# Five feed-forward slices ahead instead of three in the first block, and no attention loads in the first step of a burst

## The chip, the cores and the metric

The kernel runs as one program on one core of a Trainium2 chip. The metric is the device time of one execution in microseconds (us). The core's engines are TensorE (PE in the profile; PEld is its weight load), VectorE (DVE), ScalarE (ACT), GpSimd (POOL) and SyncE (SP, which here only issues DMAs). Each engine runs its own instructions in program order and waits on semaphores for the others.

## The reference

Chunked attention without a mask, followed by two gated feed-forward blocks. Batch, heads, sequence and head size are 8, 8, 576 and 64; the chunk is 64; there are 4608 tokens of width 512.

```python
attn = softmax(scale * q_c @ k_c^T)      # per chunk of 64 tokens and head
x = (attn @ v_c) as tokens x 512
x = ((x @ w_a) * (x @ w_b)) @ w_out      # 512 -> 1536 -> 512
x = (((x @ w1) * (x @ w2)) @ w3) @ w_o2  # 512 -> 1024 -> 1024 -> 512
```

## The kernel before, in words

The 4608 tokens are nine blocks of 512. float32 products are made of three fp32r products of parts: a weight or an activation is split into a high part (an ACT copy, line 253) and a low part (a subtraction on DVE or POOL, line 254).

The first feed-forward layer is phase 0. Its width of 1536 is cut into 12 slices `f` (`NF[0]` = 12). Slice `f` needs the pair of weights `w_a`, `w_b` and the output weights `wo`. A weight is loaded as raw doubles (`Conv.load`, line 170), turned into float32 by four operations on DVE and ACT (lines 176, 179, 182, 187: `s1` and `s2`) and split (lines 669, 673; 695, 698 for `wo`). `Pump` keeps these jobs in order, three for a slice: `w_a`, `w_b`, `wo`. The converted weights are stored to DRAM by POOL's queue (line 157): the split pair as `dw` (512 KB each), the unsplit pair as `d32` (256 KB each), `wo` as `dwo`; later blocks load them from there.

The first two blocks, T = 0 and T = 1, are done plainly, slice by slice. Before the first slice the attention of block T = 0 runs for four head pairs (`U[0]` to `U[3]`) in a software pipeline: a step `t` holds `turn` (transposes of q and k on PE, copied out by ACT), `scores`, `soft1` and `soft2` (DVE, with the exponent on ACT), `flip`, `apply` and `put`; five conversion jobs run between them. Then `plain_step` runs the slices in the order of `plain_order`: `AHEAD` slices of T = 0 alone, then T = 1's slice `f - AHEAD` before T = 0's slice `f`, then the rest of T = 1. A step of T = 0 is 24 products of 128x512 (`pa` and `pb`, line 843) and 12 of the layer's second product for the slice before (`acc`, line 886, from `wo`); a step of T = 1 has the 24 only, and its gated result waits in SBUF (`G0p`). At the points within a step a `Track` hands out pieces: the conversions (`conv`) and the attention of T = 1 (`late`) and then of the next two blocks (`at`).

After the two blocks comes a burst: the second products of T = 1, 12 steps of 12 products, each with its `wo` loaded from DRAM by `Outs.ahead`, which has four homes for them. In the burst the operands of the next pair of blocks are formed on DVE and ACT (pieces of `strassen_pieces`). Four more pairs or single blocks of phase 0 and then phase 1 follow, each with a burst.

q, k and v are not loaded where they are asked for: `ask` puts a load in a list, and `tick(loads=n)` hands the next n to SP's queue, one for each quarter of a burst step; a piece that needs its data calls `settle`, which hands out all that stand before them. SP issues in order, so a load that waits for its buffer holds up all that stand behind it.

## Time and profile before

| what | value |
|---|---|
| median of 3 runs | 1638.82 us (1638.47 to 1640.89) |
| profiled execution, its own time | 1642.08 us |
| span of the profiled execution | 1640.3 us |
| granted TensorE clock, mean over the span | 0.986 of full speed |
| HBM traffic | 268.70 MB read, 85.98 MB written |

The span runs from the first to the last instruction; its execution took 1.8 us longer than it, and lies 3.3 us above the median. In the profile's page PE is busy for 1559.8 us of the span; the part that is not is spread unevenly, so the stretches are read one by one. A timeline row gives the start, the length, the line and the operation, and in brackets the idle time ahead of it with what ended it.

### The profile page before, as it was taken

What the parts mean: (1) busy time and instruction counts of PE and PEld (TensorE: products, weight loads), DVE (VectorE), ACT (ScalarE), POOL (GpSimd) and SP (SyncE); (2) the same over time, 40 slices, a digit from 0 to 9 for tenths busy, and PEclk for the clock granted to TensorE, in tenths of its full rate; (3) what the DMA queues carried; (4) which work ended last, traced back from release to release, by engine and by line L of the source; (5) the groups of instructions that cost most, each with busy time, mean ns of one, the idle gap of its engine ahead of it and who ended that gap; (6) DMA issues with size and microseconds to landing.
All of it is one profiled execution on the core that took longest, in us unless ns stands there. A gap on an engine that the chain in (4) does not pass through costs nothing.

```text
span 1640.3 us, 24184 instructions
## 1 busy us (share of the span) xinstructions
PE 1559.8 (95%) x8968; PEld 1254.6 (76%) x8968; DVE 858.3 (52%) x1384; ACT 551.4 (34%) x989; POOL 490.5 (30%) x502
## 2 busy tenths in 40 slices
PE   4889997899998999999999899999999999999998
PEld 3668776677777777787777677888878878878887
DVE  5667756486756555476775235545542442442331
ACT  5545444222343222433234223333421321321322
POOL 1223333222243211442225112223521421421422
PEclk8899998999999999999999999999999999999999
DMA  9977844787726787379984799776366266266184
GB/s 223 291 224 248 273 154 129 227 249 229 251 85 188 202 225 228 106 223 335 343 281 164 270 313 322 307 268 247 118 223 217 75 221 221 71 216 205 67 292 155
DMA packets 277013, 356.31 MB, mean 217 GB/s; under 512 B 174240, under 2 KB 194720, under 8 KB 276896
## 3 DMA queue, kind: packets, MB, share of 16 engines
q1 hardware_dynamic: 249728, 265.63, 52.9%
q0 software_dynamic: 23616, 81.80, 13.0%
q10 hardware_dynamic: 3552, 7.34, 1.3%
q8 instruction: 71, 1.16, 0.3%
q14 instruction: 46, 0.38, 0.1%
HBM read 268.70 MB, written 85.98 MB: 216 GB/s over the span
## 4 chain that ended last, share of the span: by engine, by line
PE 78%; DVE 6%; DMA 5%; issue 3%; ACT 3%; SPq 3%; POOL 1%; DVEq 0%; POOLq 0%; ACTq 0%
PE P L857 40%; PE acc L886 21%; PE pa L843 4%; PE pb L843 4%; PE wf L1115 3%; DMA wo<-dwo 3%; SPq L148 2%; PE pb0L L843 2%; PE pa0L L843 2%; PE x L407 1%; PE s L356 1%; DVE c L945 1%; DMA qk<-in_q_dram 1%; ACT xP L253 1%; PE t L478 1%
## 5 line engine op out<-in xcount | busy, mean ns | idle before, releaser
L857 PE MATMUL P<-xP,w 128*128 128x512 f32 (+1 forms) x3066 | 704.5, 382 | 11.6 <-DVE c L945 8.6
L857 PEld LDWEIGHTS P<-xP,w 128*128 128x128 f32 x3066 | 550.4, 188 | 135.2 <-DVE c L945 13.4
L945 DVE TENSOR_TENSOR c<-P,c 128x512 f32<-128x512 f32 (+1 forms) x228 | 150.4, 662 | 332.6 <-PE P L857 331.9
L942 ACT COPY c<-P 128x512 f32<-128x512 f32 (+1 forms) x228 | 128.4, 564 | 227.4 <-PE P L857 227.1
L973 POOL TENSOR_TENSOR G<-c,c 128x512 f32<-128x512 f32 x68 | 89.7, 1319 | 332.5 <-DVE c L945 332.4
L253 ACT CAST gh<-c 128x512 fp32r<-128x512 f32 x68 | 42.2, 621 | 329.6 <-DVE c L972 329.6
L254 POOL TENSOR_TENSOR gl<-c,gh 128x512 fp32r<-128x512 f32 x68 | 90.7, 1334 | 171.7 <-ACT gh L253 171.7
L886 PE MATMUL acc<-gh,wo 128*128 128x512 f32 x384 | 138.0, 397 | 0.0
L972 DVE TENSOR_TENSOR c<-P,c 128x512 f32<-128x512 f32 x68 | 47.0, 692 | 135.1 <-PE P L857 135.0
L886 PE MATMUL acc<-wo,gh 128*128 128x512 f32 x320 | 111.1, 390 | 0.5 <-ACT gh L253 0.5
L157 POOL DMA_DIRECT2D dw<-w x58 | 32.3, 558 | 176.5 <-DVE w L254 80.2
L886 PEld LDWEIGHTS acc<-gh,wo 128*128 128x128 f32 x384 | 72.5, 189 | 15.8
L254 DVE TENSOR_TENSOR xP<-xP,xP 128x512 fp32r<-128x512 f32 (+1 forms) x56 | 65.1, 1203 | 28.1 <-ACT xP L253 28.1
L843 PE MATMUL pa<-xq,w 128*128 128x512 f32 x288 | 76.0, 416 | 0.0
L886 PE MATMUL acc<-gl,wo 128*128 128x512 f32 x192 | 75.3, 392 | 0.0
L843 PE MATMUL pb<-xq,w 128*128 128x512 f32 x288 | 71.1, 396 | 0.0
L886 PEld LDWEIGHTS acc<-wo,gh 128*128 128x128 f32 x320 | 60.1, 188 | 13.4 <-ACT gh L253 1.0
L895 ACT COPY ev<-acc 128x512 f32<-128x512 f32 x72 | 42.4, 588 | 80.0 <-PE acc L886 75.1
L843 PEld LDWEIGHTS pa<-xq,w 128*128 128x128 f32 x288 | 57.0, 201 | 13.2 <-ACT xq L253 0.3
L886 PE MATMUL acc<-wo,gl 128*128 128x512 f32 x160 | 62.7, 392 | 0.8 <-POOL gl L254 0.8
L843 PEld LDWEIGHTS pb<-xq,w 128*128 128x128 f32 x288 | 52.9, 188 | 10.8
L373 ACT ACTIVATE e<-e 128x512 f32<-128x512 f32 x36 | 22.8, 632 | 90.5 <-DVE e L367 90.5
(158 smaller groups left out, 2369.8 us busy)
## 6 DMA issues: line engine op xcount, KB each, us to landing
w<-dw SPq DMA_DIRECT2D x175, 512.0 KB, 4.6
wo<-dwo SPq DMA_DIRECT2D x128, 512.0 KB, 4.5
dw<-w POOLq DMA_DIRECT2D x58, 512.0 KB, 4.2
w<-dw SPq DMA_DIRECT2D x75, 256.0 KB, 3.8
su<-d SPq DMA_DIRECT2D x20, 512.0 KB, 5.1
x2d<-ev POOLq DMA_DIRECT2D x36, 256.0 KB, 3.7
x<-x2d SPq DMA_DIRECT2D x36, 256.0 KB, 4.7
out_dram<-ev POOLq DMA_DIRECT2D x36, 256.0 KB, 3.0
```

The source lines that it names most:

```text
L148: nc.sync.dma_start(*asks["left"].popleft())
L253: nc.scalar.copy(dst_h, src)
L254: eng_l.tensor_tensor(dst_l, src, dst_h, op=ALU.subtract)
L843: nc.tensor.matmul(ps, w[m][:, kk // 2, wp, kk % 2], xq[kk // 2][:, kk % 2, xp], start=(n == 0), stop=(n == 3 * KM - 1),)
L857: nc.tensor.matmul(ps, w[:, wp, kt], x[:, kt, xp], start=(begins and n == 0), stop=(n == 5), skip_group_check=True,)
L886: nc.tensor.matmul(acc[m], a, b, start=(f == 0 and (wp, gp) == SEQ[0]), stop=(f == NF[ph] - 1 and (wp, gp) == SEQ[-1]),)
L895: nc.scalar.copy(t, acc[m])
L942: nc.scalar.copy(t, src)
L945: add = lambda o, a, b: nc.vector.tensor_tensor(o, a, b, op=ALU.add)
L972: nc.vector.tensor_tensor(g, last, c11, op=ALU.mult)
L973: nc.gpsimd.tensor_tensor(g_place(ph, nm.split("_")[0], f, gplaces), c22, c12, op=ALU.mult)
L1115: nc.tensor.matmul(ps, t[:, gp, jj], wo2[jj // 2][:, jj % 2, wp], start=(jj == 0 and (wp, gp) == SEQ[0]), stop=(jj == NF[1] - 1 and (wp, g ...
```

## The change

Four things change. First, the start: q, k and v of `U[0]` and `U[1]` are loaded on three queues (SP, ACT, POOL), the first three weights are loaded on SP behind them and not ahead of them on ACT, and of the conversion jobs two and not five run ahead of the first slice. Second, the order of the slices: five slices of T = 0 come first, the pair weights of slices 4 and 5 stand in the homes `G1` and `G2`, and the `dw` stores of slice `f + 1` are put out in T = 1's step `f` (those of 0 and 1 in step 0). Third, PE writes the transposes of q and k in token order, every fourth column, so that ACT's copy is contiguous. Fourth, the bursts: no asked load is handed out in step 0 (`hold`), four `wo` are looked at after it, and the loads for the next pair of blocks stand among the burst's pieces and not ahead of the burst.

```diff
     def tick(every=False, loads=0):
-        settle(asks["done"] + loads)
+        settle(asks["done"] + (0 if state.get("hold") else loads))
...
                 for t in range(4):
-                    c = slice(t * P, (t + 1) * P)
-                    nc.tensor.transpose(ps[:, c], src[:, c], ident)
-                nc.scalar.copy(
-                    self.t[i].rearrange("p (i t) -> p t i", t=4),
-                    ps.rearrange("p (t i) -> p t i", t=4),
-                )
+                    nc.tensor.transpose(to[:, t], src[:, t * P : (t + 1) * P], ident)
+                nc.scalar.copy(self.t[i], ps)
...
+        def queues(self):
+            early = self.T == 0 and self.hp < 2
+            return nc.sync, nc.scalar if early else nc.sync, nc.gpsimd if early else nc.sync
...
-            t = w_tile(2 * (f % 4) + m, f"w0_{f}_{m}")
-            pairs.setdefault((0, f), {})[m] = t
+            if f in (4, 5):
+                if m == 0:
+                    tiles = pool.tile([P, 2, 2, 2, 2, P], F32R, tag=f"G{f - 3}", name=f"w0_{f}")
+                    pairs[0, f] = {i: tiles[:, i] for i in range(2)}
+                t = pairs[0, f][m]
+            else:
+                t = w_tile(2 * ((f if f < 4 else f - 6) % 4) + m, f"w0_{f}_{m}")
+                pairs.setdefault((0, f), {})[m] = t
...
-                store(dw[0][f][m], whole(t).bitcast(F32), 2, nc.gpsimd)
...
+        state["hold"] = True
         parts = [ready(ph, j, order[0], gplaces) if first is None else first]
...
                 parts.append(ready(ph, j, order[2], gplaces))
-            state["outs"].ahead(3)
+                state["hold"] = False
+            state["outs"].ahead(3 if f else 4)
...
-        for i in range(3):
-            pump.load(nc.scalar)
-        for u in U[:NHP]:
+        for n, u in enumerate(U[:NHP]):
             u.load1()
             u.load2()
-        settle(asks["all"])
+            settle(asks["all"])
+            if n:
+                pump.load()
...
-                seq += [(1, f - ahead), (0, f)]
-            return seq + [(1, f) for f in range(n - ahead, n)]
-
-        AHEAD = 3
+                upto = f - ahead + 1 if f < 9 else f - 2
+                seq += [(1, i) for i in range(done, upto)] + [(0, f)]
+                done = upto
+            return seq + [(1, f) for f in range(done, n)]
+
+        AHEAD = 5
...
-            if t in (1, 2, 4, 5, 6):
+            if t == 2:
+                pump.ahead = 0
+                pump.begin(2)
+            if t == 3:
                 pump.run()
+                pump.run()
+            if t == 4:
+                pump.flush()
+            if t == NHP + 2:
+                pump.ahead = 2
+                pump.begin(4)
...
-                conv = Track([conv_piece()] * (1 if f == 0 else 3), 5 if f + 1 < AHEAD else 8)
+                conv = Track([conv_piece()] * (4 if f == 0 else 3), 5 if f + 1 < AHEAD else 8)
...
+            if T == 1:
+                for i in [f + 1] if f else [0, 1]:
+                    for m in range(2 if i < NF[0] else 0):
+                        store(dw[0][i][m], whole(pairs[0, i][m]).bitcast(F32), 2, nc.gpsimd)
...
-                    first_sums[n_].load()
-                for n_, i in ((0, 0), (0, 3), (1, 0)):
-                    load_part(ph, orders[ph, sb][n_], i)
+                    begins_with.append((0.1, False, first_sums[n_].load))
+                for n_, i in ((0, 0), (0, 3), (1, 0), (1, 3)):
+                    begins_with.append(
+                        (0.1, False, lambda f=orders[ph, sb][n_], i=i: load_part(ph, f, i))
+                    )
+                for n_, p in enumerate(begins_with):
+                    pieces.insert(4 + 3 * n_, p)
...
-                if sb == 1:
-                    settle(units[0].qk_end)
-                    load_part(ph, orders[ph, sb][1], 3)
```

The first place is the start of SP's queue, where a name as `qk_0_256` is the q and k buffer of head pair 0 with a running number, and `cv` is a raw weight. Before:

```order
L148 DMA qk_0_256<-in_q_dram 128x4x64 x2
L148 DMA qk_0_256<-in_k_dram 128x4x64 x2
L148 DMA v_0_257<-in_v_dram 128x4x64 x2
L148 DMA qk_1_258<-in_q_dram 128x4x64 x2
L148 DMA qk_1_258<-in_k_dram 128x4x64 x2
L148 DMA v_1_259<-in_v_dram 128x4x64 x2
L148 DMA qk_2_260<-in_q_dram 128x4x64 x2
```

On the same queue now, at its start:

```order
L149 DMA qk_0_250<-in_q_dram 128x4x64 x2
L149 DMA qk_1_258<-in_q_dram 128x4x64 x2
L171 DMA cv_Y_266<-in_moe_w_a_dram 128x4x256
L149 DMA qk_2_269<-in_q_dram 128x4x64 x2
L149 DMA qk_2_269<-in_k_dram 128x4x64 x2
L149 DMA v_2_270<-in_v_dram 128x4x64 x2
L171 DMA cv_Y_266<-in_moe_w_b_dram 128x4x256
```

The k and v loads of the first two head pairs have left for ACT's and POOL's queues, and the weights that ACT issued at its start stand here between the head pairs.

The second place is POOL in the first slices; `dw` and `d` are the DRAM homes of the split and the unsplit pair, `gl` the low part that the second product waits for. Before, from the first store:

```order
L157 DMA dw_0_0_64<-w_0_0_350 128x1024
L157 DMA d_0_0_144<-cv_Y_251 128x512
L157 DMA dw_0_1_65<-w_0_1_420 128x1024
L157 DMA d_0_0_144<-cv_Y_251 128x512
L695 TENSOR_TENSOR wo_579<-cv_Y_251,wo_579 128x512
L157 DMA dwo_0_164<-wo_579 128x1024
L157 DMA dw_1_0_68<-w_1_0_629 128x1024
L157 DMA d_0_1_145<-cv_Y_251 128x512
L254 TENSOR_TENSOR gl_0_0_719<-sa_0_0_675,gh_0_0_718 128x512
```

POOL now, from its first store:

```order
L158 DMA d_0_0_144<-cv_Y_267 128x512 x2
L255 TENSOR_TENSOR gl_0_0_693<-sa_0_0_654,gh_0_0_692 128x512
L707 TENSOR_TENSOR wo_657<-cv_Y_267,wo_657 128x512
L158 DMA dwo_0_164<-wo_657 128x1024
L158 DMA d_0_1_145<-cv_Y_267 128x512
L158 DMA d_0_1_145<-cv_xo_344 128x512
L707 TENSOR_TENSOR wo_759<-cv_xo_344,wo_759 128x512
L158 DMA dwo_1_165<-wo_759 128x1024
L255 TENSOR_TENSOR gl_0_1_817<-sa_0_1_784,gh_0_1_816 128x512
```

The `dw` stores are gone from here; the first four of them stand behind the fifth slice's `gl`.

The third place is SP's queue at the end of the first burst, where `wo_0` is the last `wo` of the burst. Before:

```order
L726 DMA wo_2_3190<-dwo_2_166 128x1024
L148 DMA v_1_2900<-in_v_dram 64x2x64 x4
L726 DMA wo_1_3220<-dwo_1_165 128x1024
L148 DMA qk_2_3125<-in_q_dram 32x8x32 x4
L726 DMA wo_0_3246<-dwo_0_164 128x1024
L148 DMA qk_2_3125<-in_q_dram 32x8x32 x4
```

The same stretch now:

```order
L738 DMA wo_2_3166<-dwo_2_166 128x1024
L149 DMA qk_1_2887<-in_q_dram 32x8x32 x4
L738 DMA wo_1_3196<-dwo_1_165 128x1024
L149 DMA qk_1_2887<-in_q_dram 32x8x32 x4
L149 DMA qk_1_2887<-in_k_dram 32x8x32 x8
L149 DMA v_1_2888<-in_v_dram 64x2x64 x2
L738 DMA wo_0_3232<-dwo_0_164 128x1024
```

The attention loads run one head pair later than before, and 14 of them now stand between the last two `wo`, where there were 4.

## Rows read from the trace of the kernel before

**Rows 1.** Stretches, us: busy by PE, PEld, DVE, ACT, POOL; clock, DMA share, GB/s.

```profile
0.00:39.20 39.20, 18.38 (x304) 14.43 (x304) 23.07 (x54) 20.08 (x31) 3.48 (x11) 0.91 0.92 229
39.20:93.10 53.90, 42.43 (x412) 32.24 (x408) 35.64 (x69) 28.16 (x47) 15.22 (x19) 0.88 0.88 269
93.10:261.60 168.50, 165.12 (x1220) 132.89 (x1213) 107.00 (x180) 73.64 (x128) 51.24 (x62) 0.99 0.66 210
261.60:312.80 51.20, 41.15 (x191) 32.52 (x190) 32.49 (x45) 19.86 (x37) 19.77 (x19) 0.87 0.71 195
480.90:521.30 40.40, 37.03 (x191) 29.70 (x190) 32.31 (x38) 18.79 (x34) 20.74 (x18) 1.00 0.58 159
684.40:720.50 36.10, 36.02 (x158) 29.15 (x157) 28.75 (x27) 18.41 (x33) 21.75 (x18) 1.00 0.63 181
```

**Rows 2.** Timeline of PE, from the start to T = 1's first slice.

```profile
8.72 1.08 PE L478 MATMUL t<-ident,qk 128*128 128x128 f32 x4 [8.72 <-DMA qk<-in_q_dram]
...
39.23 4.49 PE L843 MATMUL pa<-xq,w 128*128 128x512 f32 x12
...
77.72 1.04 PE L478 MATMUL t<-ident,qk 128*128 128x128 f32 x8
...
93.11 4.61 PE L843 MATMUL pa<-xq,w 128*128 128x512 f32 x12
```

**Rows 3.** Waits of PE from 0 to 94 us: total, times, longest.

```profile
PE f L491 <- DVE e L381: 10.7, 5, 3.9
```

**Rows 4.** Timeline of DVE: its first instruction.

```profile
13.38 0.76 DVE L365 TENSOR_REDUCE mx<-s 128x4 f32<-128x256 f32 x2 [13.38 <-PE s L356]
```

**Rows 5.** Groups on DVE, 0 to 262 us: count, busy us, mean ns, idle before.

```profile
L187 DVE SCALAR_TENSOR_TENSOR cv_xo<-cv_xo,cv_xo 128x512 int32<-128x512 int32 x16 | 17.6, 1098 | 2.1 <-ACT cv_xo L182 2.1
L179 DVE SCALAR_TENSOR_TENSOR cv_xo<-cv_xo 128x512 int32<-128x512 int32 x16 | 12.0, 753 | 0.8
L381 DVE TENSOR_TENSOR e<-e,sm 128x512 f32<-128x512 f32 x16 | 12.7, 793 | 0.6
L365 DVE TENSOR_REDUCE mx<-s 128x4 f32<-128x256 f32 x32 | 12.0, 417 | 19.6 <-PE s L356 19.6
L378 DVE TENSOR_REDUCE sm<-e 128x8 f32<-128x512 f32 x16 | 10.8, 678 | 2.3 <-ACT e L373 2.3
L669 DVE TENSOR_TENSOR w<-cv_Y,w 128x512 fp32r<-128x512 f32 x13 | 8.9, 685 | 8.1 <-ACT w L673 8.1
L176 DVE TENSOR_SCALAR cv_xo<-cv_xo 128x512 int32<-128x512 uint32 x16 | 8.1, 504 | 0.0
```

**Rows 6.** Groups on ACT, 0 to 262 us, same columns.

```profile
L479 ACT COPY kT<-t 128x512 f32<-128x512 f32 x16 | 17.8, 1114 | 0.7 <-PE t L478 0.6
L494 ACT COPY pT<-f 128x512 f32<-128x512 f32 x16 | 9.5, 591 | 11.8 <-PE f L491 11.8
```

**Rows 7.** The chain that ended last: start, us, what.

```profile
133.36 2.72 PE pa L843 x12
...
289.87 2.72 PE acc L886 x12
```

**Rows 8.** Timeline of PE, the waits of the first two bursts.

```profile
283.18 0.76 PE L886 MATMUL acc<-gh_1b,wo 128*128 128x512 f32 x1 [7.40 <-DMA wo<-dwo]
...
308.35 0.51 PE L886 MATMUL acc<-gh_1b,wo 128*128 128x512 f32 x1 [2.65 <-DMA wo<-dwo]
...
518.42 0.47 PE L886 MATMUL acc<-gh_3b,wo 128*128 128x512 f32 x1 [1.55 <-DMA wo<-dwo]
```

**Rows 9.** Timeline of SP's queue, first burst.

```profile
265.03 5.61 SPq L148 DMA_DIRECT2D qk<-in_k_dram  x8
...
278.92 0.34 SPq L726 DMA_DIRECT2D wo<-dwo  x1
```

**Rows 10.** The chain again: the last `wo` of the first and second burst.

```profile
301.32 6.89 DMA wo<-dwo
...
514.23 4.06 DMA wo<-dwo
```

More of the change, by code (lines that the diff above doesn't have):

```diff
@@ L139, in chunk_attention_two_gated_products, with ask @@
     asks = {"left": deque(), "all": 0, "done": 0}
-    def ask(to, src):
-        asks["left"].append((to, src))
+    def ask(to, src, queue=None):
+        asks["left"].append((queue or nc.sync, to, src))
         asks["all"] += 1
@@ L147, in settle @@
         while asks["done"] < n and asks["left"]:
-            nc.sync.dma_start(*asks["left"].popleft())
+            queue, to, src = asks["left"].popleft()
+            queue.dma_start(to, src)
             asks["done"] += 1
     def tick(every=False, loads=0):
-        settle(asks["done"] + loads)
+        settle(asks["done"] + (0 if state.get("hold") else loads))
         for s in stores:
@@ L436, in chunk_attention_two_gated_products @@
     class TurnedOnPE(Unit):
+        def queues(self):
+            return nc.sync, nc.sync, nc.sync
         def load_qk(self):
@@ L451, in load_qk @@
                             ),
+                            self.queues()[0 if src is q else 1],
                         )
@@ L462, in load_v @@
                             hs[s : s + n, :].rearrange("(c p) d -> p c d", p=P),
+                            self.queues()[2],
                         )
@@ L475, in turn @@
             for i, (ps, src) in enumerate(zip(self.banks("t"), (self.qb, self.kb))):
+                to = ps.rearrange("p (i t) -> p t i", t=4)
                 for t in range(4):
-                    c = slice(t * P, (t + 1) * P)
-                    nc.tensor.transpose(ps[:, c], src[:, c], ident)
-                nc.scalar.copy(
-                    self.t[i].rearrange("p (i t) -> p t i", t=4),
-                    ps.rearrange("p (t i) -> p t i", t=4),
-                )
+                    nc.tensor.transpose(to[:, t], src[:, t * P : (t + 1) * P], ident)
+                nc.scalar.copy(self.t[i], ps)
         def flip_bank(self):
@@ L506, in chunk_attention_two_gated_products, with queues @@
     class First(TurnedOnPE):
+        def queues(self):
+            early = self.T == 0 and self.hp < 2
+            return nc.sync, nc.scalar if early else nc.sync, nc.gpsimd if early else nc.sync
         def slots(self):
@@ L1191, in plain_order @@
         def plain_order(ph, ahead):
-            n = NF[ph]
+            n, done = NF[ph], 0
             seq = [(0, f) for f in range(ahead)]
             for f in range(ahead, n):
-                seq += [(1, f - ahead), (0, f)]
-            return seq + [(1, f) for f in range(n - ahead, n)]
-        AHEAD = 3
+                upto = f - ahead + 1 if f < 9 else f - 2
[3 more added lines that the diff above has]
+        AHEAD = 5
         order = plain_order(0, AHEAD)
@@ L1217, in chunk_attention_two_gated_products @@
                 U[t + 1].load2()
-            if t in (1, 2, 4, 5, 6):
+            if t == 2:
+                pump.ahead = 0
+                pump.begin(2)
+            if t == 3:
                 pump.run()
+                pump.run()
[4 more added lines that the diff above has]
+                pump.begin(4)
             if t < 3:
-                pump.load(nc.scalar)
+                pump.load()
             tick(loads=8)
@@ L1234, in chunk_attention_two_gated_products @@
                 late.finish()
-                at = Track(both[cut:], 4 * (len(order) - n) - 2)
+                at = Track(both[cut:], sum(3 if T_ else 5 for T_, _ in order[n:]) - 3)
             def point(pe=True):
@@ L1386, in chunk_attention_two_gated_products @@
             if ph == 0 and sb == 1:
+                begins_with = []
                 for n_ in range(2):
                     first_sums[n_] = summed(ph, orders[ph, sb][n_], n_)
-                    first_sums[n_].load()
-                for n_, i in ((0, 0), (0, 3), (1, 0)):
-                    load_part(ph, orders[ph, sb][n_], i)
+                    begins_with.append((0.1, False, first_sums[n_].load))
[5 more added lines that the diff above has]
+                    pieces.insert(4 + 3 * n_, p)
                 pieces = pieces + first_sums[0].pieces()
```

## The prediction

> **What bounds the kernel now.** PE is busy for 1559.8 us of the span, so the question is where the other 80 us are. I read the stretches first [rows 1]: from slice to slice of the two plain blocks, between 93.1 and 261.6 us, PE is busy for 165.1 of 168.5 us at a clock of 0.99, and nothing is to be had there. Three stretches are different. Ahead of the first slice it is busy for 18.4 of 39.2 us; in the three slices that T = 0 runs alone for 42.4 of 53.9 us, and then at a clock of 0.88; in the first burst for 41.2 of 51.2 us. The third burst has the same second products and no wait: 36.1 us.
>
> The timeline of PE says what begins and ends them [rows 2]: the first transpose waits for q until 8.72 us, the first slice starts at 39.23, T = 1's first slice at 93.11. The list of waits names the softmax on DVE as the longest of PE's releasers besides that first q, 10.7 us in 5 waits [rows 3]. DVE itself starts at 13.38 us [rows 4] and is busy for 23.07 of the 25.8 us until 39.2. So the start is a load and then a DVE chain; the lone slices are a chain of PE, ACT and DVE that neither engine fills (DVE is busy for 35.6 of 53.9 us, 66%). In the bursts PE waits for `wo`, 7.40 and 2.65 us in the first and 1.55 in the second [rows 8]; SP's queue shows why the first is late: it issues 8 loads of k in 5.61 us, more of v behind them, and the `wo` only at 278.92 [rows 9].
>
> **The change, part by part.** *Start.* Before, 1.5 MB of weights and 0.5 MB of q and k had to land for the first transpose: 2.0 MB at the 229 GB/s of the stretch is 8.7 us, as seen. Now q and k of the first head pair share the DMA only with v and the next q and k, some 1.25 MB: 5.5 us, a gain of 3.2. Two ACT copies of a turn lie on the chain; contiguous they should take what the flip's copy takes, 0.59 for 1.11 us [rows 6]: 1.0. Of the conversions ahead of the last softmax three `s1` (lines 176 and 179, 0.50 + 0.75) and two `s2` (line 187, 1.10) go, 6 us of DVE by the means [rows 5]; I take 4, because these means hold the long cases of later slices. The first slice then starts at 39.2 - 3.2 - 1.0 - 4 = 31 us (28 if all 6 count and the pipeline tightens, 36 if `w_b`, which now lands behind 3.25 MB, about 14 us, holds DVE up).
>
> *Five lone slices.* Demands until T = 1's first slice. DVE: a set of three conversions is 3 x (0.50 + 0.75 + 1.10) + 2 x 0.69 = 8.4 us; five sets are 42 (two jobs are done by the start, 17 are needed by the time T = 1 begins). Four head pairs of attention at 0.68 + 0.79 + three times two half-size instructions of 0.375 + 0.4 for two small ones = 4.1 each are 16.5. Five gated products are 3.4. That is 62 us, and 56 if back-to-back starts save what the 23.07 busy us of the first stretch suggest; I take 58. PE: five slices at 2 x 2.72 and four second products at 2.72 [rows 7] are 38.1; attention is 3.3 per head pair (165.1 busy us less 12 x 5.44 and 9 x 8.16, over eight), so 13.2: 51 us. DMA: until 93.1 us 9.0 + 14.5 = 23.5 MB moved; seven `dw` stores of 0.5 MB leave, two slices with 2.5 MB each of loads, `d32` and `dwo` come: 25 MB, which at 229 and then 269 GB/s end at 98.7 us. DVE at the 0.9 that it reached between 13.4 and 39.2 us gives 31 + 58 / 0.9 = 95 us. All three are near full; I take 95, between 87 (56 us without idle time) and 99. Attention has 25 points now for what had 15, which is why I expect 0.9 and not the 0.66 of before. By 95 us two slices more are done, each 5.44 + 2.72 = 8.16: the gain is 93.1 + 16.3 - 95 = 14.4 us.
>
> *Rest of the two blocks.* The `dw` stores come here: 12 MB in all. T = 1's first step and the slice behind it (16.3 us with attention) meet four of them, 2 MB, with 1.5 MB of weights, 1 MB of other stores and 0.5 MB of attention: 307 GB/s, above the 269 seen. The buffers of slice 0's weights are written again only for slice 6, so most of this is hidden: 1 us (0 to 4).
>
> *Transposes in every fourth column.* 128 of them in the span, eight in 1.04 us, 0.13 each [rows 2]. No row shows PE writing with a stride. Nearest is ACT, whose strided copy takes 1.11 for 0.59 us, 1.9 times [rows 6]; that much on 0.13 is 0.12 x 128 = 15 us, the upper bound; the lower is 0. A transpose of 128 columns takes more than twice what a product takes for as many (2.72 / 12 / 4 = 0.057 us), so its output is slow enough to hide a halved rate: 2 us. The Trainium skill (SBUF — State Buffer, Door 1: The DMA port swizzle) says that PSUM has lines of 8 bytes and that a non-contiguous PSUM access pattern significantly slows matmuls. By that rule the term would lie near the upper bound; no row of this trace shows it.
>
> *First burst.* SP is free when it starts, and `wo_7` goes out as its home comes free, about 2.9 us in. But the asked loads now start one step late and were not handed out ahead, and those of the second head pair are forced by its `turn`: 14 stand before `wo_0`. Ahead of `wo_0` stand 44 asked loads, 8 `wo` and 6 others. At 0.65 us (0.70 in rows 9, where the queue was fuller), 0.4 and 0.37 that is 34 us; with 2.9 to start and 1 for a home it goes out at 37.8 us and lands after 4.1 [rows 10] at 41.9. The last step (2.72) ends at 44.6, and with half the clock behind a wait of 6 us, as behind the 7.40, at 46.6: 4.6 us less than 51.2. Bounds: 13.7 less if no `wo` is late (36.1 and 1.4 for scores), 1.8 less if the landing takes 6.89.
>
> *Second burst.* The same forcing adds 8 asked loads before the last `wo`: 8 x 0.55 = 4.4 us, of which 1.5 fall into time that SP waited for homes. The wait of 1.55 becomes 4.4, and half the clock behind it costs 1.5: 4.4 us more (0 to 7). The third burst has no attention pieces and stays at 36.1; later bursts issue each `wo` when its home comes free, before and now.
>
> Sum: -14.4 + 1 + 2 - 4.6 + 4.4 = -11.6 us on the profiled 1642.1, so 1630.5; that execution lies 3.3 above the median, so 1627 for the median.
>
> **The rivals.** *The hold works as it reads (chance 0.22).* The first burst loses all its waits, 13.7 us, and the second keeps its 1.55: -14.4 + 3 - 13.7 = -25, a median of 1614. For it: the 7.40 us wait comes from asked loads alone [rows 9]. Against it: the 14 loads before `wo_0`.
>
> *DVE fills no better than before (0.13).* If the lone slices keep DVE at 0.66, 58 us of work take 88, T = 1 begins at 119 and not 95, the first part loses 9.5 us, and with the other terms the median is 1651, slower. It decides at 0.77: from there on, with T = 1 later than 106.6 us, nothing is left. For it: the softmax waits [rows 3] and a mean of 1.10 us for line 187, which waits for something in many cases; against it: 25 points, and 0.89 at the start. The Trainium skill (SBUF — State Buffer, Who interferes with whom) has DVE instructions with two SBUF inputs blocked by a POOL instruction that reads SBUF. By that rule, line 187 with its 1.10 us against 0.69 for line 669 agrees in part, and five slices bring five `gl` and five `wo` on POOL.
>
> *The strided transposes cost what the skill's rule says (0.10).* 15 us in place of 2 give a median of 1640, no faster. It decides at 0.10 us for each transpose.
>
> *The lead is given back (0.08).* The DMA, not DVE, sets the lone slices, and the moved `dw` stores are late for slices 6 and 7: T = 1 at 99, 4 us in the rest, the bursts as forecast: -10.4 + 4 + 2 = -4.4, and another 3 lost wherever it is: within 0.2%.
>
> **How the numbers follow.** The forecast has 0.47: 1627, by itself 1619 to 1634. The range goes to the first rival at its low end and to the strided transposes at its high end, 1612 to 1640; outside lie the DVE rival and the tails. About 0.2% (3.3 us) is what a measurement here can tell from no change. Faster by more than that: 0.22 of the first rival, 0.46 of the forecast, 0.08 of the others, 0.76. Slower: the DVE rival's worse part and a tail of the transposes, 0.13. The rest is 0.11.
>
> **What the changed profile would show.** Right: first transpose near 5.5 us; first `pa` near 31; T = 1's first `pa`, the one behind five slices, near 95, with DVE near 0.9 busy in between; ACT's copies of the turn near 0.6; eight transposes in some 1.1 us; the first burst near 47 us long with its last wait before `wo_0`; a second-burst wait of about 4. Wrong: a first burst of 38 us (the hold works), eight transposes in 2 us, or T = 1 beyond 105 us.

## The result: slower by 0.5%, where 0.7% faster was forecast

The changed kernel takes 1648.12 us (median of 4 runs, 1646.42 to 1649.75), the kernel before 1639.86 in the runs beside it: a ratio of 1.0054, 95% interval 1.0038 to 1.0069. The profiled execution took 1649.75 us, 7.7 more than the one of before. Its stretches, in the columns of [rows 1]: start, five lone slices, rest of the two blocks, first burst, stretch to the second burst, second burst, third burst.

```profile
0.00:35.30 35.30, 19.51 (x304) 16.41 (x304) 19.00 (x46) 14.53 (x27) 5.00 (x12) 0.85 0.95 224
35.30:107.00 71.70, 58.72 (x485) 45.79 (x480) 56.56 (x101) 34.93 (x66) 25.64 (x29) 0.91 0.85 258
107.00:259.50 152.50, 147.57 (x1150) 118.23 (x1140) 84.00 (x154) 58.90 (x113) 42.77 (x54) 1.00 0.62 200
259.50:311.50 52.00, 41.87 (x189) 32.47 (x190) 33.85 (x48) 19.37 (x35) 20.77 (x20) 0.90 0.75 213
311.50:484.50 173.00, 162.75 (x1118) 127.55 (x1117) 113.89 (x215) 49.77 (x94) 44.61 (x48) 0.99 0.69 207
484.50:530.00 45.50, 39.60 (x190) 31.63 (x189) 32.23 (x38) 18.88 (x35) 21.75 (x19) 0.92 0.63 169
692.50:731.20 38.70, 36.84 (x159) 29.09 (x158) 28.86 (x27) 18.54 (x33) 21.40 (x18) 1.00 0.71 190
```

The timeline of PE has the places of [rows 2] and [rows 8] again (first transpose, first slice, a wait in the first lone slice, T = 1's first slice, the `wo` waits of the first two bursts):

```profile
6.75 1.94 PE L484 MATMUL t<-ident,qk 128*128 128x128 f32 x8 [6.75 <-DMA qk<-in_q_dram]
...
35.34 4.45 PE L855 MATMUL pa<-xq,w 128*128 128x512 f32 x12
...
48.07 1.39 PE L484 MATMUL t<-ident,qk 128*128 128x128 f32 x8 [4.02 <-issue]
...
107.06 3.12 PE L855 MATMUL pa<-xq,w 128*128 128x512 f32 x12
...
278.36 0.47 PE L898 MATMUL acc<-gh_1b,wo 128*128 128x512 f32 x1 [1.87 <-DMA wo<-dwo]
284.07 0.66 PE L898 MATMUL acc<-gh_1b,wo 128*128 128x512 f32 x1 [2.71 <-DMA wo<-dwo]
306.06 0.76 PE L898 MATMUL acc<-gh_1b,wo 128*128 128x512 f32 x1 [5.40 <-DMA wo<-dwo]
524.49 0.77 PE L898 MATMUL acc<-gh_3b,wo 128*128 128x512 f32 x1 [4.16 <-DMA wo<-dwo]
```

Read down the two views: the first slice starts 3.9 us earlier than before, T = 1's first slice 13.95 later, with two slices (16.3) done ahead of it, so 2.4 us are won by then, and 2.0 by the first burst. From there the change loses: 0.8 in the first burst (52.0 for 51.2), 4.9 in the stretch behind it (173.0 for 168.1, between the bursts of [rows 1]), 5.1 in the second burst, 2.6 in the third. The fourth burst gives 2.4 back (39.5 us).

Between 35 and 107 us the list of DVE's waits (total, times, longest) has one large row: DVE stands at the gated product of a lone slice until PE has done that slice's `pb`.

```profile
DVE sa L1011 <- PE pb L855: 11.1, 4, 4.2
```

In the three lone slices of before (39.2 to 93.1 us) the same row was

```profile
DVE sa L999 <- PE pb L843: 3.6, 3, 1.8
```

In the first burst SP's queue is no longer late at its start, as it was in [rows 9]; it is full in the middle:

```profile
262.65 0.35 SPq L738 DMA_DIRECT2D wo<-dwo  x1
263.05 2.06 SPq L149 DMA_DIRECT2D qk<-in_q_dram  x2
265.27 0.85 SPq L775 DMA_DIRECT2D su<-d  x2
266.17 3.15 SPq L149 DMA_DIRECT2D qk<-in_q_dram  x4
269.43 1.78 SPq L753 DMA_DIRECT2D w<-dw  x1
271.25 1.44 SPq L149 DMA_DIRECT2D qk<-in_q_dram  x2
274.73 0.34 SPq L738 DMA_DIRECT2D wo<-dwo  x1
...
295.31 5.24 SPq L149 DMA_DIRECT2D qk<-in_k_dram  x8
300.59 1.69 SPq L149 DMA_DIRECT2D v<-in_v_dram  x2
302.38 0.54 SPq L738 DMA_DIRECT2D wo<-dwo  x1
```

Twelve microseconds lie between two `wo`: eight asked loads (6.7 us), the two `su` (unsplit weights for sums, from `d`) and one `w` that the change put there (2.6), and 2.8 us in which SP issued nothing. The last `wo` goes out at 302.38, behind the 14 loads of `qk` and `v` that the prediction counted.

In the stretch behind the burst the asked loads and `su` are late for DVE, at places where DVE had no wait for a DMA before:

```profile
400.44 0.71 DVE L346 STREAM_TRANSPOSE kT<-qk 128x512 f32<-128x512 f32 x1 [1.55 <-DMA qk<-in_k_dram]
...
413.76 0.42 DVE L783 TENSOR_TENSOR su<-su 128x256 f32<-128x256 f32 x1 [1.38 <-DMA su<-d]
```

### The profile page after: what moved, and what is told of

It reads as the page before. It is cut to its first block, busy times and chain, and to the rows that moved or that the text cites. A ratio compares the mean times of both kernels' runs of the same rounds, so it can differ in the third digit from the quotient of the medians.

```text
span 1647.9 us, 24180 instructions
## 1 busy us (share of the span) xinstructions
PE 1561.8 (95%) x8968; PEld 1257.7 (76%) x8968; DVE 850.7 (52%) x1384; ACT 537.2 (33%) x989; POOL 493.9 (30%) x506
## 4 chain that ended last, share of the span: by engine, by line
PE 75%; DVE 8%; DMA 6%; issue 4%; ACT 3%; SPq 2%; POOL 1%; DVEq 0%; POOLq 0%; ACTq 0%
PE P L869 38%; PE acc L898 19%; PE pa L855 4%; PE pb L855 4%; PE wf L1129 3%; DMA wo<-dwo 2%; SPq L149 2%; PE pb0L L855 2%; PE pa0L L855 2%; PE x L408 1%; DMA w<-dw 1%; PE s L357 1%; DVE c L957 1%; DMA su<-d 1%; PE t L484 1%
## 5 line engine op out<-in xcount | busy, mean ns | idle before, releaser
L869 PE MATMUL P<-xP,w 128*128 128x512 f32 (+1 forms) x3066 | 703.5, 382 | 15.3 <-DVE c L957 11.1
L907 ACT COPY ev<-acc 128x512 f32<-128x512 f32 x72 | 42.3, 587 | 86.7 <-PE acc L898 82.3
L855 PEld LDWEIGHTS pa<-xq,w 128*128 128x128 f32 x288 | 56.2, 201 | 14.4 <-DVE w L682 1.6
```

Of the source, the lines that this page charges most:

```text
L855: nc.tensor.matmul(ps, w[m][:, kk // 2, wp, kk % 2], xq[kk // 2][:, kk % 2, xp], start=(n == 0), stop=(n == 3 * KM - 1),)
L869: nc.tensor.matmul(ps, w[:, wp, kt], x[:, kt, xp], start=(begins and n == 0), stop=(n == 5), skip_group_check=True,)
L907: nc.scalar.copy(t, acc[m])
```

## The experiments

Sixteen kernels were run (e8 stands in the text alone); each ratio is to the kernel before on the same chip, with its 95% interval. The stage times (us, from the profile of each: first slice, T = 1's first slice, begin of the first burst, first burst, stretch behind it, second and third burst) carry more than the sums. The changed kernel, e1, e2 and e9 have the same slices ahead of the first burst, and yet begin it at 259.6 to 261.5 us and T = 1 at 107.1 to 109.0; so a difference of under 2 us between the stages of two profiles tells nothing by itself, and the 2.4 and 2.0 us above are the best of these four:

| kernel | ratio (interval) | first `pa` | T = 1 | burst 1 at | burst 1 | stretch | burst 2 | burst 3 |
|---|---|---|---|---|---|---|---|---|
| before | 1 | 39.2 | 93.1 | 261.6 | 51.2 | 168.1 | 40.4 | 36.1 |
| changed | 1.0054 | 35.3 | 107.1 | 259.6 | 52.0 | 173.0 | 45.5 | 38.7 |
| e1_no_hold | 0.9972 (0.9955 to 0.9988) | 36.1 | 109.0 | 261.5 | 46.2 | 168.5 | 39.9 | 36.1 |
| e2_old_burst | 0.9940 (0.9919 to 0.9961) | 36.0 | 108.9 | 261.4 | 42.4 | 169.7 | 42.4 | 36.1 |
| e3_ahead3 | 1.0088 (1.0065 to 1.0111) | 35.4 | 94.9 | 266.7 | 51.5 | 169.8 | 43.8 | 37.8 |
| e4_old_turn | 1.0061 (1.0039 to 1.0083) | 36.6 | 109.5 | 262.4 | 52.4 | 173.2 | 44.8 | 38.5 |
| e5_old_start | 0.9943 (0.9928 to 0.9959) | 39.8 | 106.6 | 259.5 | 43.7 | 168.0 | 41.4 | 35.8 |
| e6_before_hold | 1.0017 (1.0001 to 1.0033) | 39.8 | 94.6 | 263.7 | 42.0 | 168.1 | 45.4 | 38.5 |
| e7_order3 | 0.9975 (0.9964 to 0.9986) | 35.4 | 93.7 | 264.6 | 47.8 | 169.4 | 40.1 | 36.1 |
| e9_hold_only | 1.0008 (0.9994 to 1.0021) | 35.5 | 108.4 | 261.0 | 42.1 | 174.5 | 45.2 | 39.2 |
| e10_dw_early | 0.9951 (0.9938 to 0.9964) | 35.1 | 107.7 | 260.3 | 42.5 | 168.0 | 40.3 | 36.1 |
| e11_low_pool | 0.9964 (0.9951 to 0.9976) | 36.0 | 111.3 | 263.9 | 42.9 | 168.1 | 42.3 | 36.0 |
| e12_homes3 | 1.0023 (1.0011 to 1.0035) | 36.1 | 94.8 | 265.2 | 49.4 | 167.9 | 40.3 | 36.2 |
| e13_order_only | 0.9978 (0.9965 to 0.9990) | 39.3 | 106.0 | 258.8 | 45.4 | 168.2 | 39.9 | 35.9 |
| e14_order4 | 1.0012 (0.9996 to 1.0027) | 39.1 | 102.4 | 267.8 | 42.1 | 168.1 | 41.5 | 37.1 |
| e15_less_dve | 0.9908 (0.9894 to 0.9922) | 35.4 | 103.0 | 255.5 | 43.3 | 168.0 | 42.6 | 36.0 |
| e16_v_act2 | 0.9966 (0.9953 to 0.9979) | 40.1 | 112.2 | 264.8 | 42.8 | 169.5 | 41.4 | 37.3 |

### The burst edits: e1, e2, e6, e9

e1_no_hold takes the hold out of the changed kernel; e9_hold_only keeps it and puts the inserted loads back ahead of the burst; e2_old_burst does both; e6_before_hold puts the hold alone into the kernel before.

```diff
-        state["hold"] = True                       # e1, e2 (e6 adds these lines)
-                state["hold"] = False
-            state["outs"].ahead(3 if f else 4)
+            state["outs"].ahead(3)
...
-                    begins_with.append((0.1, False, first_sums[n_].load))      # e2, e9
+                    first_sums[n_].load()
...
-                    pieces.insert(4 + 3 * n_, p)
+                    load_part(ph, orders[ph, sb][n_], i)
...
+                    settle(units[0].qk_end)
+                    load_part(ph, orders[ph, sb][1], 3)
```

> The changed kernel without the hold: asked loads are handed out in step 0 of a burst again, and three wo are looked at after it as before; the loads inserted among the burst's pieces stay. Theory 1 (late asked loads): the hold shifts all asked loads by one step, so the 14 in front of the last wo and the late q and k behind the burst come from it: the second burst goes back from 45 to about 40.5 us, the stretch between the bursts from 173.4 to 168.5, the last wait of the first burst from 5.4 to below 3, the median to about 1637. Rival (inserted loads): the five loads in the middle of the first burst fill SP's queue and the DMA and the asked loads are late because of them: the bursts and the stretch between stay within 1 us of the changed kernel in sum, median 1646 to 1648.

> The changed kernel with every burst edit undone (no hold, three wo after step 0, the loads for the next pair ahead of the burst): start, slice order and transposes of the change alone. Theory (the burst edits lose all of it): the first burst starts near 259 as in the changed kernel, from there on the times of the kernel before: about 1637, 3 us faster than before. Rival (the moved dw stores or the strided transposes disturb the bursts): the second burst stays near 45 us and the median above 1643.

> The kernel before with the hold alone (no asked load in step 0 of a burst, four wo looked at after it). Theory (asked loads one step late are the loss, whatever stands around them): the second burst near 44 to 45 us, the third near 38, the stretch between the first two 3 to 5 us longer, while the first burst gains some of its 7.4 us wait; in sum 3 to 9 us slower, 1.002 to 1.0055. Rival (the hold does harm only with the inserted loads): first burst shorter, the others as before, 0.995 to 0.999.

> The changed kernel with the hold, but the loads for the next pair ahead of the burst as before (the inserted loads alone undone). Theory (the hold shifts the asked loads to the second and third bursts whatever stands around it, the inserted loads cost the first burst and the stretch behind it): first burst 42 to 44 us, stretch to the second burst 168 to 170, second burst near 45 and third near 38.5: 1.000 of the kernel before, between the changed kernel (1.0054) and the one with the old burst (0.994). Rival (the two edits do harm only together): first burst near 42, second near 41, third 36: 0.994.

Without the hold (e1) the second and third burst and the stretch are back at the times of before:

```profile
261.50:307.70 46.20, 40.56 (x189) 32.11 (x190) 33.64 (x47) 19.36 (x35) 20.59 (x19) 0.93 0.73 213
307.70:476.20 168.50, 161.14 (x1118) 126.34 (x1117) 115.65 (x215) 49.67 (x94) 44.92 (x48) 1.00 0.72 214
476.20:516.10 39.90, 37.12 (x190) 29.78 (x189) 32.14 (x38) 18.87 (x35) 21.32 (x18) 1.00 0.57 161
678.70:714.80 36.10, 35.98 (x158) 29.27 (x157) 28.83 (x27) 18.54 (x33) 21.50 (x18) 1.00 0.64 184
```

With the hold and without the inserted loads (e9) the first burst has no wait for `wo`, and the three other stretches have the losses of the changed kernel:

```profile
261.00:303.10 42.10, 38.52 (x189) 31.10 (x190) 35.05 (x47) 19.38 (x35) 20.35 (x19) 0.96 0.64 185
303.10:477.60 174.50, 164.21 (x1116) 128.56 (x1116) 113.75 (x215) 49.84 (x94) 45.20 (x49) 0.98 0.69 208
477.60:522.80 45.20, 40.01 (x190) 31.91 (x190) 32.30 (x38) 18.84 (x34) 21.30 (x18) 0.92 0.61 156
685.50:724.70 39.20, 36.66 (x158) 29.12 (x157) 28.71 (x27) 18.56 (x34) 21.72 (x18) 1.00 0.71 188
```

So the four kernels with the new start and slice order form a square: 0.9940 with neither edit, 0.9972 with the inserted loads, 1.0008 with the hold, 1.0054 with both. The hold costs 0.7 to 0.8% (11 to 13 us), the inserted loads 0.3 to 0.5%, and they add up; the rivals (inserted loads alone, or both only together) fall. In the first burst alone they do not add up: 42.4 us with neither, 42.1 with the hold, 46.2 with the inserted loads, 52.0 with both. In the kernel before (e6) the hold does what its lines say, the first burst falls from 51.2 to 42.0, and most of it goes again: 5.0 in the second burst, 2.4 in the third. The ratio, 1.0017, has nothing left of it. There the stretch behind the first burst kept its 168.1, against the expectation; only with the new slice order does it grow (e9, changed). Why only there stays open.

e2 went further than expected (0.9940 for some 0.998): its first burst lost its waits for `wo` altogether, without a burst edit.

### Where the first burst's gain comes from: e7, e12, e10, e13

```diff
-        AHEAD = 5            # e7, e12 (on e2); e3 on the changed kernel
+        AHEAD = 3
...
-            if f in (4, 5):                                     # e12 only
-                    tiles = pool.tile([P, 2, 2, 2, 2, P], F32R, tag=f"G{f - 3}", name=f"w0_{f}")
...
-                t = w_tile(2 * ((f if f < 4 else f - 6) % 4) + m, f"w0_{f}_{m}")
+            t = w_tile(2 * (f % 4) + m, f"w0_{f}_{m}")
...
+                store(dw[0][f][m], whole(t).bitcast(F32), 2, nc.gpsimd)    # e10, e13
```

> The changed kernel with the old burst edits and three slices ahead in place of five. Theory (the new slice order is worth its gain in the first burst: the weights' homes come free earlier, so SP gets past the loads for the next pair and to the wo): the first burst has its wait of some 7 us for wo again and is near 50 us, and starts 4 to 7 us later than with five: median near 1645, 1.003. Rival (the gain in the first burst comes from the moved dw stores): first burst near 42 without such a wait, median near 1638, 0.998.

> The changed kernel with the old burst edits, three slices ahead, and the homes of the pair weights as before (no weights in G1 and G2). Theory (the two extra homes let SP load the next pair's weights earlier and reach the wo): with the old homes SP waits for PE's last reads until 250 to 260 again, the first wo goes out near 278 and the first burst has its wait of 5 to 7 us back, near 51 us: median near 1641, 1.001. Rival (the first burst's gain with three slices ahead, 47.8 for 51.3, is from the moved dw stores): the burst stays at 48 us, 0.9975.

> The changed kernel with the old burst edits and the dw stores put out behind their conversion again, not at the second block's turn. Theory (the stores are 0.5 MB each, seven of them fall into the lone slices, where DVE, ACT and PE are one chain and the DMA is at 0.85): T=1's first slice 0 to 3 us later than 108.9, the first burst as with the late stores (no wait of 7 us), since the homes decide that: 0.994 to 0.996. Rival (the late stores free or hold the weights' homes): the wait of SP for dw, 14 us ahead of 247, goes, and the first burst comes out differently by over 3 us.

> Of the change only the slice order with its two extra homes and the transposes: start, conversions, dw stores and bursts as before. Theory (the order and the homes are the whole gain): 0.994 to 0.995, the first burst near 43 us and its start within 2 us of 260. Rival (start, late stores and order need each other): 0.997 or more.

SP's queue ahead of the first burst (`w` are weights of the next pair, line 753 and 755, whose homes must be free) in e2, and the first `wo` behind them:

```profile
247.42 0.32 SPq L753 DMA_DIRECT2D w<-dw  x1
248.63 0.32 SPq L755 DMA_DIRECT2D w<-dw  x1
250.24 0.32 SPq L753 DMA_DIRECT2D w<-dw  x1
...
260.60 0.34 SPq L755 DMA_DIRECT2D w<-dw  x1
...
269.15 0.41 SPq L738 DMA_DIRECT2D wo<-dwo  x1
```

and in e12, with three slices ahead and the homes of before:

```profile
254.08 0.32 SPq L753 DMA_DIRECT2D w<-dw  x1
264.43 0.32 SPq L755 DMA_DIRECT2D w<-dw  x1
...
274.37 0.43 SPq L755 DMA_DIRECT2D w<-dw  x1
282.54 0.38 SPq L738 DMA_DIRECT2D wo<-dwo  x1
```

The first `wo` goes out 7.8 us behind the burst's begin in e2 and 17.3 in e12, as in the kernel before (17.3, [rows 9]), and e12 has the wait of before again (7.33 us, 7.40 in [rows 8]). e7 differs from it by the two homes alone: SP waits for PE's reads of the old weights for 1.7 and 1.3 us, in e12 for 2.6 and 9.9; the first `wo` goes out 7.5 us into the burst, the burst takes 47.8 us with one wait of 2.83, and the ratio falls from 1.0023 to 0.9975. So the extra homes in `G1` and `G2` free the others earlier, and SP passes its blocked loads and reaches the `wo`. The 5.4 us from there to e2 (42.4) come with the two further slices; as the first `wo` is no earlier in e2, and the granted clock is 0.96 there and 0.89 in e7, how they come is not shown.

The homes are half of the matter. Before, SP's queue ahead of the first `wo` at 278.92 [rows 9] has

```profile
259.44 0.32 SPq L743 DMA_DIRECT2D w<-dw  x1
...
260.28 4.71 SPq L148 DMA_DIRECT2D qk<-in_q_dram  x8
...
271.18 6.45 SPq L148 DMA_DIRECT2D v<-in_v_dram  x10
```

The row at 259.44 had waited 7.7 us for PE's last reads, one ahead of it 16.2. Behind it come 28 asked loads, 17.9 us of issuing. e2 has the same 28 loads, and begins them 9.7 us earlier. e6 keeps the waits for the homes (16.1 and 7.7 us); its hold takes 12 of the 28 loads from ahead of the first `wo`, which goes out 10.0 us into the burst, and the burst takes 42.0 us. So each of the two cures the first burst without the other, and where the slice order had done it the hold had nothing left to gain there (e9, 42.1).

With five slices the moved stores have no part in the first burst: e10 puts them back and keeps 42.5 us and T = 1 at 107.7. e13 puts the old start back as well, and comes to 0.9978, its rival's figure, where e5 (old start, late stores) has 0.9943, e10 (new start, early stores) 0.9951 and e2 (both new) 0.9940. So neither the old start nor the early stores cost anything clear of the intervals alone, and the two together cost some 0.3%. Where, the stages don't show: in the lone slices of e13 the DMA share is 1.00 (0.92 in e5), but its profiled execution, 1630.3 us, is the fastest of its twelve runs (to 1640.6).

### The start and the lone slices: e3, e5, e14, e15, e11, e8, e16

e5_old_start puts the loads, conversions and queues of the old start back into e2. e14_order4 is e13 with `AHEAD = 4`.

> The changed kernel with three slices ahead in place of five, everything else of it kept. Theory (the two extra lone slices return almost nothing: T=1's first slice comes at 107.1, and two slices less would have it about 28 us earlier for 16 us of work moved back behind it): T=1's first slice near 85 us and the first burst near 262, so 3 us slower than the changed kernel, 1651. Rival A (five are worth the 14 us of the prediction's count): first burst near 270, 1660. Rival B (five slices are a loss): first burst before 256, 1645.

> The changed kernel with the old burst edits and also the start of the kernel before (three weights and the later ones on ACT first, q, k and v on SP, five conversion jobs ahead of the first slice, one piece in step 0); the order of five slices and the transposes of the change stay. Theory (the 3.9 us of the start are only moved: the conversions left out there stand in the lone slices, where DVE is the chain): first slice near 39, T=1's first slice within 1.5 us of 108.9, first burst near 261.5 and the median within 2 us of the kernel with the new start, 0.994 of the kernel before. Rival (the start is a gain of its own): T=1's first slice and the median 3 to 4 us later, 0.996 to 0.997.

> The same with four slices ahead. Theory 1 (each further lone slice returns part of its time, some 1.6 us at the first burst's start as from three to five): 1 to 2 us behind five, 0.995 to 0.996. Theory 2 (with DVE, ACT and PE in one chain the fifth returns nothing): equal to five within 1 us.

e5 has its first slice 3.8 us later than e2 and T = 1's first slice 2.3 us earlier, and the two ratios are equal (0.9943, 0.9940): the start's gain is given back within five slices. In these DVE is busy for 51.95 us in e5 and 56.56 in e2; PE's clock differs too (0.95, 0.87), and what each of the two does is not separated. e3 shows the same from the other side: three slices ahead with the new start take 59.5 us (58.3 in e7) where the kernel before needs 53.9 [rows 1], with DVE busy for 40.75 us and not 35.64, and T = 1 begins at 94.9. Five against three slices are worth 7.1 us at the first burst with the burst edits (266.7, 259.6), between theory and rival A, and 3.2 without them (e7 264.6, e2 261.4), though the slices ahead of the burst are the same. With four (e14) the lone slices take 63.4 us, three less than the five of e13 (66.7), and the ratio is 1.0012 for 0.9978, so neither of its theories held (the burst begins 9.0 us later, but e13's profile is of its fastest run): the T = 1 attention has to be done within the lone slices, four or five, and the fifth takes 3.3 us more in all.

e15 leaves the first operation of the conversion out for 15 weights (their values are not the reference's), e11 moves a subtraction from DVE to POOL:

```diff
-            nc.vector.tensor_scalar(                             # e15, weights 3 to 17
-                self.lo, self.lo.bitcast(U32), 2.0**-29, 7.0, op0=ALU.mult, op1=ALU.min
-            )
...
-                nc.vector.tensor_tensor(by_part(t, 1), v2, by_part(t, 0), op=ALU.subtract)
+                (nc.gpsimd if 0 < f < 5 else nc.vector).tensor_tensor(          # e11
```

> The changed kernel with the old burst edits, without the first operation of the conversion (shift of the low words, 0.42 us) for the 15 weights behind the first two; their low words are replaced by others, so the weights of the first slices are not the reference's. 6.3 us of DVE leave the lone slices and nothing takes their place. Theory 1 (DVE's work sets the lone slices, at a fill of 0.8): T=1's first slice 6 to 8 us earlier, 101 to 103, median 0.990 to 0.991. Theory 2 (DVE and PE wait for each other in program order, whatever the length of DVE's instructions): T=1's first slice under 2 us earlier, 107 or later, median 0.993 to 0.994.

> The changed kernel with the old burst edits, and the subtraction that makes the low part of the pair weights on POOL and not on DVE for slices 1 to 4: eight instructions of 0.69 us, 5.5 us, leave DVE in the lone slices. Theory 1 (DVE's work sets the lone slices at a fill of 0.8): T=1's first slice comes 5 to 7 us earlier, 102 to 104, median 0.990 to 0.991. Theory 2 (they are a chain over PE, ACT and DVE in which DVE itself waits for pb, 11 us in the changed kernel): POOL's 1.3 us in place of 0.69 lengthens the chain, T=1's first slice within 1.5 us of 108.9 or later, median 0.994 to 0.996.

The lone slices of e15 in the columns of [rows 1], and DVE's longest wait in them:

```profile
35.40:102.90 67.50, 56.78 (x484) 44.37 (x480) 50.71 (x86) 34.68 (x66) 24.53 (x29) 0.93 0.90 270
```

```profile
DVE sa L1013 <- PE pb L857: 13.1, 5, 4.5
```

They are 5.3 us shorter than e2's (67.6 for 72.9 us) for 5.9 us less of DVE (50.71 for 56.56), so DVE's work is on the path nearly one for one, as theory 1 has it. A part can be the clock, 0.93 here and 0.87 in e2; but the changed kernel runs e2's slices at 0.91 in 71.7 us, still 4.2 more, and the ratio is 0.9908 for e2's 0.9940, some 5 us. The fill, however, is no better (50.71 of 67.5 us, 0.75), and the waits for `pb` are as long as in e2 (12.5 us). DVE's amount and its waits add up, because the gated product stands in DVE's order between the conversions. In e11 5.5 us left DVE and T = 1 came 2.4 us later than in e2; the last section shows what grew in their place.

```diff
+            late = self.T == 1 and self.hp < 2                    # e8, e16, on e2
-            return nc.sync, nc.scalar if early else nc.sync, nc.gpsimd if early else nc.sync
+            return nc.sync, nc.scalar if early else nc.sync, nc.gpsimd if early else nc.scalar if late else nc.sync
```

> The changed kernel with the old burst edits, and v of the first two head pairs of T=1 on ACT's queue and not on SP's. Theory 1 (in the first lone slice PE waits 4.0 us for a q that SP issues late, behind 12 loads of v in 8.5 us): q goes out near 35 and not 43, the transposes at 48 lose their wait, T=1's first slice comes 3 to 4 us earlier, near 105, median 0.992. Theory 2 (DVE, ACT and PE are one chain there, and a wait removed in one place comes back in another): T=1's first slice within 1 us of 108.9, median 0.994.

> The changed kernel with the old burst edits, and all loads of v for the first two head pairs of T=1 on ACT's queue (the run before of this name's kind had left them on SP, since they are cut at the edge of a batch and go through another function). Theory 1 (the raw weights, which SP issues behind 8.5 us of v, are late for DVE in the first lone slice): w_a of slice 2 goes out 8 us earlier, T=1's first slice comes 2 to 4 us earlier, near 105 to 107, median 0.992 to 0.993. Theory 2 (the 4.0 us in front of the transposes at 48 us is DVE's softmax, which stands behind the gated product of the slice, and this one waits for pb): the 4.0 us stay, T=1's first slice within 1 us of 108.9, 0.994 to 0.995.

e8 (0.9945, 0.9925 to 0.9965) moved only a few of the loads, SP still issued 12 of `v` from 33.24 on, so it tells nothing. e16 moved them: `w_a` of slice 2 went out at 36.1 (41.9 in the changed kernel), but PE's 4.0 us stayed, and the lone slices took 72.1 us. ACT, where the loads of `v` now stood, had the first slice begin at 40.1, so T = 1's came at 112.2, later than either theory has it. So the loads on SP are not what holds the lone slices. What fits the 4.02 us at 48.07 is DVE: its softmax of the scores ran from 46.90 to 48.3, behind the gated product that had waited for `pb` until 43.54, and the transposes began within it. That releaser is not in the trace, so this is argued, not shown.

### The transposes: e4

> The changed kernel with the transposes written to PSUM as before (contiguous) and copied out by ACT with a stride. Theory (the strided write costs PE nothing, the copy gains 0.5 us each): eight transposes take 1.03 to 1.06 us in both, the first slice starts 1 to 2 us later, the median is 0 to 3 us above the changed kernel. Rival (the strided write costs PE): the transposes take less than 1.0 us per eight, and the median falls by up to 15 us.

Matmul of one transpose and ACT's copy of `kT`, by tile, between 100 and 262 us (count, then shortest, median and longest in ns): the changed kernel, and e4 with the old way:

```profile
L484 PE MATMUL t<-ident,qk x64: 272/273/273, 101.3 to 229.5; 128*128 128x128 f32 x64
...
L485 ACT COPY kT<-t x8: 585/592/605, 102.6 to 229.9; 128x512 f32<-128x512 f32 x8
```

```profile
L484 PE MATMUL t<-ident,qk x64: 272/273/273, 103.7 to 232.3; 128*128 128x128 f32 x64
...
L485 ACT COPY kT<-t x8: 1117/1122/1153, 105.4 to 233.1; 128x512 f32<-128x512 f32 x8
```

The strided write costs PE nothing, the contiguous copy saves 0.53 us, and the median does not tell the two kernels apart. The first eight transposes take 1.94 us in both (at 6.75 and 7.21 us), so these long ones, which the prediction named as a sign of being wrong, are not from the write.

The fastest versions of the reference's computation are e2 (0.9940) and e5 (0.9943), some 10 us faster than the kernel before and 18 than the changed one.

## Why the prediction was wrong, step by step

For the profiled execution -11.6 us were forecast and +7.7 measured. Of these 19.3 us, 9.4 are missing by the first burst's begin, 5.4 in it, 0.7 in the second burst and 3.8 behind, in stages that the sum left out.

**Start: 3.9 us for 8.2.** The first transpose came at 6.75 us (5.5 forecast), the copies take 0.59 as forecast, DVE's busy time ahead of the first slice fell by 4.1 us (4 forecast), and the first slice began at 35.3, within the bounds. So of the 5 us for copies and conversions 1.9 arrived; what took the others no run shows (the granted clock is 0.85 in this stretch, 0.91 before). The step after it does count the moved conversions; e5 and e3 show that they take back what the start gains.

**Five lone slices: 2.4 us for 14.4 by T = 1's first slice, the start's share included. This is the first step that failed.** The slices themselves were to take 64 us and took 71.7. DVE's amount was right (56.6 us for 58), the fill was not: 0.79 for 0.9, with T = 1's first slice at 107.1 for 95, beyond even the point (106.6) from which the second rival said that nothing is left. The 0.9 was taken from a stretch in which no slice ran. In a lone slice DVE waits in its own order for PE's `pb` (11.1 us), and its work adds to that (e15). PE's amount was too low as well: 51 us, counted at the full clock, where PE was busy for 58.7 at a granted 0.91. How much of DVE's wait is PE's clock and how much the order of the two engines stays open; e2 has the same slices at 0.87, and the wait is 12.5 us.

**Rest of the two blocks: 152.4 us for 152.2 of before, less than the 1 us allowed.** **Transposes: 0 for 2 us.** The rule of the Trainium skill (SBUF — State Buffer, Door 1: The DMA port swizzle) that a non-contiguous PSUM access slows matmuls is not borne out by these float32 transposes: 273 ns both ways, and the rival that rested on it falls.

**First burst: +0.8 us for -4.6. The second step that failed.** The last `wo` went out 42.8 us into the burst and not 37.8. The first one went out 3.1 us in (2.9 forecast), and the 44 asked loads took 28.7 us, 0.65 each as priced, with the 14 ahead of the last `wo` as counted; but the six other loads took 3.8 us for 2.2, and SP issued nothing for 4.3 us between all these loads where 1 was allowed. The last `wo`'s product waited 5.40 us (6 forecast). What the step did not see is in SP's rows ahead of 261 us, which it did not read: there SP waited for the homes of the next pair's weights, and the asked loads stood behind that. The new slice order frees the homes, and without any burst edit the first burst takes 42.4 us (e2; 45.4 in e13, with the old start and stores too) for 51.2. The inserted loads took that back, 3.8 us without the hold (e1) and 9.9 with it.

**Second burst: +5.1 us for +4.4, its wait 4.16 for 4.4.** This step was right, and e6, e9 and e1 show its cause, the hold.

**What the sum left out:** the stretch behind the first burst (+4.9) and the third burst (+2.6, forecast unchanged). The hold shifts all later loads, not those of two bursts alone. Of the rivals, "DVE fills no better" had the right engine, with a fill between its 0.66 and the forecast's; that it came nearest in time (1651) is luck, as T = 1 began at 107.1 and not at its 119, and the rest was lost in the bursts. "The hold works as it reads" is refuted by e6, where it works in the first burst and loses the gain in the next ones, and by e9, where nothing is left to gain in the first and the losses stay.

## What to carry to other kernels

A load that is held back to let another pass does not vanish: SP's queue has the same work one step later, and the bursts behind pay for it, so sum the queue over all bursts before moving anything in one. Before reordering loads look for what blocks the queue's head: the slice order with its two more homes did for the first burst what the hold does (42.4 and 42.0 us), and two cures of one wait don't add up. And a fill that an engine reached in one stretch holds only for that stretch's order of waits; work moved from a serial start into a stage in which the same engine is on the path is not saved.

## What the runs showed of the hardware

POOL at work beside it slows DVE. In e11 eight subtractions (5.5 us) left DVE, and yet DVE was busy for 58.09 us in the lone slices with 93 instructions, against 56.56 with 101 in e2, while POOL went from 25.61 to 37.08. The same instruction of the conversion, between 36 and 111 us, in e2 and then in e11 (count, busy us, mean ns, idle before):

```profile
L180 DVE SCALAR_TENSOR_TENSOR cv_xo<-cv_xo 128x512 int32<-128x512 int32 x8 | 5.5, 692 | 0.3
```

```profile
L180 DVE SCALAR_TENSOR_TENSOR cv_xo<-cv_xo 128x512 int32<-128x512 int32 x8 | 7.8, 971 | 0.5
```

and one with a single tensor as input, likewise:

```profile
L177 DVE TENSOR_SCALAR cv_xo<-cv_xo 128x512 int32<-128x512 uint32 x8 | 3.4, 419 | 0.0
```

```profile
L177 DVE TENSOR_SCALAR cv_xo<-cv_xo 128x512 int32<-128x512 uint32 x8 | 5.6, 703 | 0.0
```

The Trainium skill (SBUF — State Buffer, Who interferes with whom) says that a DVE instruction with two SBUF inputs contends with a POOL instruction that reads SBUF. The rows of line 180, with two such inputs, agree with it: 0.28 us more on the mean. Line 177 has one such input and grew by as much, which that sentence does not cover. In e11's timeline the slow ones are those that begin within a POOL subtraction: line 188 at 52.67 us takes 1.78 us, with one on POOL from 52.32 for 1.58, and line 177 at 70.61 takes 1.55, with one from 70.59 for 1.29; with none beside them these lines take 0.69 and 0.42.
